# A linear-attention and soft-MoE kernel: the first key half in two 64-partition loads, the second as GpSimd's first load, phi on ScalarE's queue, and a last weight piece of three rows

## The chip, the core and the metric

One core of one Trainium2 chip. The core has TensorE (PE, matmuls), VectorE (DVE), ScalarE (ACT), GpSimd (POOL) and SyncE (SP, here only DMA issues), with 16 DMA engines shared by the queues of SP, ScalarE and GpSimd. The metric is device microseconds of one execution; times below are in microseconds unless they say otherwise.

## The reference

Two stages. The first is linear attention with a state per head (batch 4, 8 heads, 768 steps, head size 48); the second a soft mixture of experts over its output (3072 tokens of width 384, 8 experts of 4 slots, inner width 1024).

```python
for t in range(S):                       # r, k, v: [4, 8, 768, 48] fp32; w, u: [8, 48]
    cur = np.einsum('bhd,bhe->bhde', u[None] * kt, vt)
    y[:, :, t] = np.einsum('bhd,bhde->bhe', rt, state + cur)
    state = w[None, :, :, None] * state + np.einsum('bhd,bhe->bhde', kt, vt)
# x: y with heads joined, [3072, 384]
logits = x @ phi                         # [3072, 32]
d = softmax(logits, axis=0)              # over tokens
slot_input = d.T @ x                     # [32, 384]
slot_out[e] = relu(slot_input[e] @ w1[e]) @ w2[e]
out = softmax(logits, axis=1) @ slot_out # [3072, 384] fp32
```

## The kernel before

The sequence of 768 is cut into six chunks of 128 steps (`c` in names), and each chunk is worked with two pairs of batches (`bl`) and two halves of heads (`hf`). Every step is a named task of a class `Plan`: it has an engine, the tasks it depends on, and the buffers that it takes and frees. A long string `ORDER`, written out, says in which order the tasks are issued, in which buffer, and for tasks that may run on several engines on which (`/A` ScalarE, `/D` VectorE, `/P` GpSimd). Each engine runs its instructions in that order.

The names that matter here: `qk`, `qr`, `qv` copy a loaded key, r or v tensor into padded form (L222 is the copy on ScalarE, L224 that on VectorE); `tk`, `tr`, `tv` transpose it on TensorE (L376); `ek`, `er`, `ev` write it out of the accumulators with the decay tables (L386); `A`, `M` are the scores and their mask; `Y` the output of a chunk; `zt`, `ze` build the decay tables from `lnw`, the logarithm of w. After the last chunk, `h` and `ht` compute the experts' hidden layer, and `o00` to `o70` the second product, one expert after the other into one accumulator (L743).

Loads. All of r, k, v and the expert weights come through GpSimd's queue, which casts fp32 to bf16 on the way: `iL2` to `iL35` are halves (two batches) of a chunk's tensor, in the order k, r, v; then `iW0` to `iW7` the first weights and `iV0` to `iV7` the second. At most eight of these loads are outstanding: from `iL10` on each waits for the one eight before it. The second weights go into the buffers of r, k and v, once these have been copied. Only the first chunk's key (`iL0` and `iL1`) comes as fp32, by SP and ScalarE into `k0`, and the copies `qk00` and `qk01` cast it.

The last expert's second weight comes in two pieces: `Va7` with the first rows and `Vb7` with the last `YL` rows (of the eight that lie on each partition). `o70` uses the first piece; then `so1` copies the sum so far (on VectorE, L224). The first four output tiles (`p0` to `p3`, L788) start from `so1`, and have the last rows' share added by `pg0` to `pg3` (L795), which multiply the gathered hidden values `gG` (L756, evicted by `gE`) with `Vb7`'s rows directly. `o76` adds the same rows to the accumulator, and `so2` copies it for the tiles from the fifth on. Tiles are scaled and evicted (`oe`, L803 on ScalarE and L805 on VectorE) and stored by SP (`dm`, L811).

`WARM` puts filler matmuls (L826, results unused) behind named tasks; `fill` (L245) does so at the start.

Of the kernel before, what the change touches and what calls it, by code (L numbers as in the profile page):

```python
# [24 lines left out]
Y000:0,0 kn01:/D Y001:2 iL24 A011:0,0 iL25 s01:4,3,1 x000:/A M011 x001:/A tk20:0,0 iL26 ev10:/A X00:2,0 pr10:0/P
S111 A100:0,1 kn11:/A tk21:1 ek20 tr20:3,0 xT00:/A M100 bv10:5,2 qv2:0/A bv11:0,3 iL27 tr21:2 ek21 iL28 pr11:/D
bk20:1,1 iL29 vn10:/A er21 iL30 kn20:/A er20 s10:5,2,2 iL31 vn11:/A qk3:1/D tv20:1,0 iL32 S110 bk21:3,2 dv01:1 S200
D1:0,1 kn21:/A ev20:/D s11:4,5,3 S201 ds1:/A tv21:1 iL33 pr20:0/D Y011:3 iL34 ev21:/A Y010:0,1 S210 A101:0,0 iL35
pr21:/D l00:2 x010:/A bv20:4,0 iW0 M101 x011:/A D2:1,0 dv10:0 bv21:0,1 vn20:/A X01:3,1 lg00:/D ds2:/A A110:0,2 S211
vn21:/A qr3:0/D iW1 Y100:2,2 xT01:/A M110 iW2 Y101:4 x100:/A iW3 l01:1 s20:5,0,0 x101:/A lg01:/D iW4 mx0 X10:3,0  # L30
sb0:0/D S301 A111:0,1 ex0:0 iW5 S300 xT10:/A tk30:2,1 dv11:1 M111 c0:1 tk31:4 cT0:/A l10:0 ek31 qv3:1/A A200:0,0
iW6 Y111:5 ek30 iW7 Y110:3,3 M200 dv20:0 lg10:/A bk30:1,0 x111:/A s21:4,2,1 x110:/A kn30:/A tr30:0,1 dv21:1 S311
tr31:5 S310 X11:3,1 qk4:0/A A201:0,1 er30 tv30:1,1 M201 tv31:2 bk31:4,1 ev30:/A Y200:0,4 ev31:/D A210:0,2 xT11:/A
zu qr4:1/D Y201:1 x200:/D kn31:/A iV0 bv30:2,2 M210 bv31:3,3 x201:/A vn30:/A l11:0 X20:4,0 vn31:/D A211:0,0 xT20:/A
Y210:1,5 lg11:/D er31 tk40:2,0 M211 pr30:0/P x210:/A tk41:3 s30:0,4,2 qv4:0/A ek40 A300:0,1 Y211:5 ek41 iV1 l20:1
S401 bk40:2,2 x211:/A pr31:/P M300 tr40:3,0 lg20:/A kn40:/A X21:4,1 tr41:5 er40 xT21:/A A301:0,2 tv40:1,0 er41
qk5:1/A D3:2,1 M301 l21:3 iV2 bk41:4,0 tv41:5 pr40:0/P lg21:/A ds3:/A ev40:/D kn41:/A A310:0,0 s31:3,2,3 gm0
ev41:/A M310 gt0:1 dv30:0 qr5:0/A bv40:4,0 bv41:5,1 S410 mx2 iV3 vn40:/A mx1 Y301:3 S400 pr41:/P vn41:/A gr00
Y300:4,6 S411 A311:0,2 gd0 x300:/D x301:/A s40:0,1,0 M311 X30:5,0 dv31:1 tk50:2,1 xT30:/A D4:3,0 S500 A400:0,1 ek50
gb0:4 ds4:/A tk51:0 iV4 gx0 Y311:5 M400 sb1:1/P qv5:1/A gs0:/P Y310:3,7 l30:2 ek51 A401:0,2 dv40:0 tr50:4,1 x310:/A  # L40
x311:/D tr51:0 ex1:1 lg30:/D M401 X31:3,1 ge0 tv50:5,1 iV5 dp0:2 dv41:1 er50 ev50:/A er51 A410:0,0 xT31:/D
s41:4,5,1 pr50:0/P M410 c1:0 Y401:3 cT1:/A S511 A411:0,2 S501 tv51:0 iV6 M411 Y400:5,0 pr51:/P ev51:/A Y410:1,1
acc0 A500:0,1 S510 x401:/A Y411:2 x410:/A M500 x400:/A bv50:0,2 x411:/A D5:4,1 iVa7 X40:3,0 vn50:/D ds5:/A A501:0,0
sb2:0/D xT40:/A bv51:1,3 M501 dv50:0 l31:5 ex2:0 l40:2 vn51:/A X41:4,1 lg31:/D mx3 A510:0,2 lg40:/D sb3:1/D xT41:/A
c2:0 dv51:1 M510 Y500:3,2 cT2:/A Y501:5 ex3:1 l41:2 x500:/D A511:0,1 iVb7 x501:/A Y510:1,3 lg41:/A M511 X50:4,0
x510:/A c3:0 xT50:/A gm1 Y511:3 mx4 cT3:/A gt1:5 gl0:2 sb4:0/D x511:/D l50:1 ex4:0 gr10 X51:4,1 lg50:/A gr20 c4:0
gq1 gd1 xT51:/D cT4:/A gb1:3 gl1 F0 F1 gx1 gs1:/D gr21 ge1 gf1:/P l51:5 gq2 gg1 dp1:1 gd2 lg51:/D am1:/P mx5
sb5:1/D ex5:1 gb2:4 F2 F3 F4 acc1 gx2 gs2 gf2:/P ge2 gg2 am2:/D dp2:0 F5 F6 acc2 un1 un0 rv:3 h10:2 rw h11:5
hs10:/A h00:1 hs11:/D h01:4 hs00:/D ht1:0 hs01:/A c5:3 hT1:/D ht0:2 cT5:/A gG0:5 hT0:/D rs:1 gE0:/A gG1:4 rr o00:0
gE1:/A o10 o20 o30 o40 o50 F7 F8 F9 o60 F10 F11 F12 F13 F14 F15 o70 F16 F17 F18 so1 p0a:3 p0b:2 p1:5 pg0a pg0b pg1  # L50
oe0a oe0b o76 p2:1 oe1 dm00 pg2 so2:/A p3:4 dm01 pg3 oe2 p4:3 p5:2 oe3 p6:5 dm02 oe4 p7:0 p8:1 oe5 oe6 p9:4 dm03
p10:3 oe7 oe8 p11:2 dm04 p12:5 oe9 oe10 p13:0 dm06 p14:1 oe11 oe12 p15:4 p16:3 oe14 oe13 p17:5 dm10 p18:2 oe16 oe15
p19:1 p20:0 oe18 oe17 p21:3 dm14 p22:4 oe20 p23:2 oe21 oe22 oe23 oe19 dm20
"""


# [49 lines left out]
def kernel(  # L106
# [123 lines left out]
    def load_rkv(y):  # L230
        x, bb = divmod(y, 2)
        c, which = divmod(x, 3)
        src = (k, r, v)[which].rearrange("(bb bl) h (c p j) d -> c bb (bl h) p (j d)", bb=2, bl=2, p=RR, j=JJ)
        O(pool.dma_start(out=raw_t(x)[:, bb * JJ * D:(bb + 1) * JJ * D], in_=src[c, bb]))  # L234
# [16 lines left out]
    k_src = k.rearrange("(bb bl) h (c p j) d -> c bb (bl h) p (j d)", bb=2, bl=2, p=RR, j=JJ)
    O(act.dma_start(out=w_r[:, :, 0:D], in_=w[:, None, :].to_broadcast([H, 2, D])))
    for bb, q in ((0, sp), (1, act)):
        O(q.dma_start(out=k0[:, bb * JJ * D:(bb + 1) * JJ * D], in_=k_src[0, bb]))
    O(act.preload_act_table_set("natural_log_exp_and_others"))
# [8 lines left out]
    O(pool.affine_select(out=ident_f[:], in_=ident_f[:], compare_op=ALU.not_equal, fill=1.0, base=0,
                         pattern=[[-1, 128]], channel_multiplier=1))
    for t in rp_r:
        O(pool.memset(t[:, :, :, D:], 0.0))
# [592 lines left out]
```

## Time and profile before

| | |
|---|---|
| time, median of 3 runs | 117.49 (117.24 to 117.93) |
| the profiled execution | 117.38, span 115.6 from the first to the last instruction |
| TensorE busy | 98.7 (85%), granted clock 0.978 |
| VectorE busy | 89.8 (78%) |
| ScalarE busy | 76.7 (66%) |
| GpSimd busy | 66.4 (57%) |
| loaded by GpSimd's queue | 19.27 MB written |
| HBM | 39.38 MB read, 4.72 MB written |

A row of the timeline or of the groups gives start, duration, engine, source line, operation, what it writes and reads, and in brackets the idle time ahead of it with what ended it. A row of a table by stretches gives the stretch and its length, the busy time of PE, PEld (weight loads), DVE, ACT and POOL, each with its number of instructions, and then the granted clock, the mean busy share of the DMA engines and GB/s. A row of the DMA list gives the KB of one load and the median time from issue to landing.

### The profile page before, as it was taken

Reading aid. Unit: us, or ns where it says so; the run is one execution under the profiler, and the core shown is the slowest. Engines: PE = TensorE matmul, PEld = TensorE weight load, DVE = VectorE, ACT = ScalarE, POOL = GpSimd, SP = SyncE. Lnnn points to the kernel's source line nnn. Section 1 sums busy time; section 2 is a strip of 40 time slices with the busy share of each in tenths; the row PEclk is TensorE's granted clock in tenths of the full one; section 3 lists DMA queues with packets and bytes.
Section 4 is the critical chain, followed back from the end, with each engine's and each line's share of the span. In section 5 each row is a group of like instructions: output and inputs, shape, how many; then the busy total and the mean of one; then the engine's idle time right before and its main releaser. Section 6 shows DMA issues by size and latency. Waiting matters only on the chain.

```text
span 115.6 us, 3911 instructions
## 1 busy us (share of the span) xinstructions
PE 98.7 (85%) x1649; PEld 76.0 (66%) x1649; DVE 89.8 (78%) x178; ACT 76.7 (66%) x124; POOL 66.4 (57%) x85
## 2 busy tenths in 40 slices
...
DMA  2999999999999999999999999999999997059994
GB/s 36 268 197 206 207 205 210 205 206 208 208 210 201 229 219 208 218 219 212 210 220 215 210 220 210 214 219 212 215 223 208 217 209 149 17 208 404 408 438 174
DMA packets 9137, 25.08 MB, mean 217 GB/s; under 512 B 1184, under 2 KB 6176, under 8 KB 8992
## 3 DMA queue, kind: packets, MB, share of 16 engines
q0 software_dynamic: 7344, 19.27, 85.7%
...
q10 hardware_dynamic: 168, 0.40, 1.4%
...
HBM read 39.38 MB, written 4.72 MB: 381 GB/s over the span
## 4 chain that ended last, share of the span: by engine, by line
PE 48%; DMA 17%; DVE 11%; ACT 9%; POOL 5%; issue 3%; DVEq 0%; ACTq 0%; POOLq 0%
DMA w_all<-in_moe_w_dram 17%; PE pG L376 9%; PE pA L415 4%; PE pG L788 3%; ACT rp L222 3%; PE pG L397 3%; PE pA L826 3%; PE pG L743 3%; PE pG L633 2%; PE pG L716 2%; PE pG L516 2%; PE pG L551 2%; POOL w_all L237 2%; PE pG L490 2%; PE pG L496 2%
## 5 line engine op out<-in xcount | busy, mean ns | idle before, releaser
L421 DVE TENSOR_TENSOR AT<-pA,mask 128x1024 bf16<-128x1024 f32 x24 | 29.2, 1218 | 1.3 <-PE pA L415 1.1
L376 PE MATMUL pG<-ident,rp 128*128 128x128 bf16 x288 | 22.5, 235 | 2.6 <-DVE rp L224 2.4
L376 PEld LDWEIGHTS <-rp 128*128 128x128 bf16 x288 | 19.2, 106 | 3.8 <-issue 2.8
L428 POOL TENSOR_TENSOR pr<-kT,rT 128x1024 bf16<-128x1024 bf16 x8 | 17.0, 2130 | 5.1 <-DVE rT L386 4.6
L445 POOL TENSOR_TENSOR dv<-vn,ds 128x768 bf16<-128x768 bf16 x12 | 17.7, 1482 | 3.0 <-DVE sd L540 2.2
L222 ACT COPY rp<-raw 128x1536 bf16<-128x1536 bf16 x11 | 16.3, 1479 | 2.6 <-PE pG L376 2.3
L222 ACT COPY vT<-pG 128x1024 bf16<-128x1024 bf16 x8 | 8.0, 1015 | 5.2 <-PE pG L376 5.2
L474 DVE TENSOR_TENSOR S<-pG,W 128x384 bf16<-128x384 f32 x20 | 10.5, 548 | 0.5 <-PE pG L466 0.5
L803 ACT ACTIVATE w_all<-pG,rcs 128x384 f32<-128x384 f32 (+1 forms) x12 | 5.8, 587 | 6.1 <-PE pG L795 5.9
L415 PE MATMUL pA<-rT,kT 64*128 64x128 bf16 x192 | 9.5, 218 | 0.3 <-DVE AT L421 0.2
L386 DVE TENSOR_TENSOR kT<-pG,Tk 128x1024 bf16<-128x1024 bf16 x12 | 8.0, 684 | 1.7 <-PE pG L376 1.3
L222 ACT CAST x<-pG 128x384 bf16<-128x384 f32 x19 | 8.5, 487 | 0.8 <-PE pG L498 0.5
L222 ACT COPY xT<-pG 128x768 bf16<-128x768 bf16 x10 | 8.0, 804 | 1.3 <-PE pG L516 1.2
L496 PE MATMUL pG<-vn,AT 128*128 128x48 bf16 x192 | 8.7, 183 | 0.2 <-ACT kn L222 0.2
L222 ACT COPY vn<-pG 128x768 bf16<-128x768 bf16 x10 | 8.0, 815 | 0.9 <-PE pG L397 0.9
L805 DVE TENSOR_SCALAR w_all<-pG,rcs 128x384 f32<-128x384 f32 (+1 forms) x13 | 6.9, 596 | 1.6 <-PE pG L795 1.6
L234 POOL DMA_DIRECT2D raw<-in_v_dram x12 | 6.3, 537 | 3.1 <-DMA raw<-in_r_dram 3.0
L386 DVE TENSOR_TENSOR rT<-pG,Tr 128x1024 bf16<-128x1024 bf16 x12 | 7.9, 683 | 0.0
L498 PE MATMUL pG<-dv,ident 128*128 128x384 bf16 x24 | 7.7, 323 | 0.0
L222 ACT COPY kn<-pG 128x768 bf16<-128x768 bf16 x9 | 7.3, 812 | 0.5 <-PE pG L397 0.5
L415 PEld LDWEIGHTS <-kT 64*128 64x128 bf16 x192 | 5.7, 94 | 2.8 <-issue 1.1
L496 PEld LDWEIGHTS <-AT 128*128 128x128 bf16 x192 | 7.1, 96 | 0.4 <-issue 0.4
...
## 6 DMA issues: line engine op xcount, KB each, us to landing
...
raw<-in_r_dram POOLq DMA_DIRECT2D x12, 192.0 KB, 7.2
raw<-in_v_dram POOLq DMA_DIRECT2D x12, 192.0 KB, 6.8
raw<-in_k_dram POOLq DMA_DIRECT2D x10, 192.0 KB, 7.2
...
out_dram<-w_all SPq DMA_DIRECT2D x4, 192.0 KB, 2.0
```

The source lines that it names most:

```text
L222: O(act.copy(dst, src))
L234: O(pool.dma_start(out=raw_t(x)[:, bb * JJ * D:(bb + 1) * JJ * D], in_=src[c, bb]))
L376: O(pe.transpose(o[:, :, j, :], rp_r[W[rp]][:, jh * JH + j].rearrange("p b d -> p (b d)"), ident[:]))
L386: O(dve.tensor_mul(dst, src, (Tk, Tr)[which][:, None, jh].to_broadcast(BC)))
L415: O(pe.matmul(pA[:, bb, h4 * C:(h4 + 1) * C], kt[s, bl, h].rearrange("p a x -> p (a x)"), rt[s, bl, h].rearrange("p a x -> p (a x)"), star ...
L421: O(dve.tensor_mul(AT_r[W[f"AT{key}"]][:], pA[:].rearrange("p bb (h t) -> p bb h t", t=C), mask[:, None, None, :].to_broadcast([128, 2, H ...
L428: O(op(e).tensor_mul(pr_r[W[f"pr{c}"]][:, bl], kT_r[W[f"kT{c}"]][:, bl].rearrange("p h j x -> p h (j x)"), rT_r[W[f"rT{c}"]][:, bl].rearra ...
L445: O(op(e).tensor_mul(dv_r[W[f"dv{c}{bl}"]][:], vn_r[W[f"vn{c}{bl}"]][:], ds_r[W[f"ds{c}"]][:, bl, :, :, None].to_broadcast([128, H, 2, D])))
L474: O(dve.tensor_mul(S_r[W[new]][:, s], bank(kb[hf])[:, 0:HD].rearrange("p (h b d) -> p h b d", b=2, d=D), W128[:, s, :, None].to_broadcast( ...
L496: O(pe.matmul(o[:, z:z + D], AT_r[W[at]][:, bb, h4, :], vn[:, hf * H2 + h4, bb, :], start=(c == 0 and h4 == 0 and bb == 0), stop=False, sk ...
L498: O(pe.matmul(o[:, 0:HD], ident[:], dv_r[W[f"dv{c}{bl}"]][:, hf * H2:(hf + 1) * H2] .rearrange("p h b d -> p (h b d)"), start=False, stop= ...
L805: O(dve.tensor_scalar(out=dst, in0=src, scalar1=rcs[:, i:i + 1], scalar2=None, op0=ALU.mult))
```

## The change

The first key half comes in two loads of 64 partitions, one from SP and one from ScalarE, still as fp32. The second half becomes GpSimd's first load and is cast on the way, as the later ones. phi moves from SP's queue to ScalarE's, behind w. The padding memsets of `rp` move from GpSimd to VectorE. The last weight piece has three rows in place of two, so there are three gathered rows (`gG0` to `gG2`), and `o70` has five rows in place of six. The fillers behind `o50`, `o60` and `o70` go from 3, 6, 3 to 1, 5, 2. `ORDER` is a different one throughout, with copies, products and evictions divided differently between the engines. A dependency makes the second weight of the first expert wait for `qk01`, and another puts `o40` behind the gathers.

```diff
-WARM = [("gl1", 2), ("gb2", 3), ("dp2", 2), ("o50", 3), ("o60", 6), ("o70", 3)]
+WARM = [("gl1", 2), ("gb2", 3), ("dp2", 2), ("o50", 1), ("o60", 5), ("o70", 2)]
...
-zt3 zc iL6 zt1 ze3 iL7 zw:0 zt0 ze1 iL8 zb ze0 iL9 zt2 qk00:0/A za zd:/D ze2 qk01:/D iL10 tk00:0,0 tk01:1 qr0:1/A
+zt0 zc iL6 za ze0 iL7 zt1 iL8 qk00:0/D ze1 zt2 qk01:/A iL9 zt3 ze2 zw:0 tk00:0,0 iL10 zb ze3 tk01:1 qr0:1/D iL11
...
-    k0 = early[:, 2560:2560 + 2 * JJ * D]
+    k0 = early[:, 2560:2560 + JJ * D]
...
     k_src = k.rearrange("(bb bl) h (c p j) d -> c bb (bl h) p (j d)", bb=2, bl=2, p=RR, j=JJ)
+    for bl, q in ((0, sp), (1, act)):
+        O(q.dma_start(out=k0[64 * bl:64 * bl + 64], in_=k_src[0, 0, 8 * bl:8 * bl + 8]))
     O(act.dma_start(out=w_r[:, :, 0:D], in_=w[:, None, :].to_broadcast([H, 2, D])))
-    for bb, q in ((0, sp), (1, act)):
-        O(q.dma_start(out=k0[:, bb * JJ * D:(bb + 1) * JJ * D], in_=k_src[0, bb]))
+    O(act.dma_start(out=phi_f[:], in_=moe_phi.rearrange("(p mo) s -> p mo s", mo=nM)))
...
-    O(sp.dma_start(out=phi_f[:], in_=moe_phi.rearrange("(p mo) s -> p mo s", mo=nM)))
     O(sp.dma_start(out=u_r[:, :, 0:D], in_=u[:, None, :].to_broadcast([H, 2, D])))
...
+    for x in range(1, 6):
+        load_rkv(x)
+    fill(3)
     for t in rp_r:
-        O(pool.memset(t[:, :, :, D:], 0.0))
-    load_rkv(2)
-    load_rkv(3)
-    load_rkv(4)
-    load_rkv(5)
-    fill(3)
+        O(dve.memset(t[:, :, :, D:], 0.0))
...
-    YL = 2
+    YL = 3
...
-            P.add("i" + name, "POOL", lambda e, f=fns[kind], x=x: f(x), deps=[lands[n - 8]] if n >= 10 else [])
+            P.add("i" + name, "POOL", lambda e, f=fns[kind], x=x: f(x), deps=[lands[n - 8]] if n >= 9 else [])
...
-                    e, rp_r[W[rp]][:, :, bb, 0:D], k0[:, bb * JJ * D:(bb + 1) * JJ * D].rearrange("p (j d) -> p j d", j=JJ)),
+                    e, rp_r[W[rp]][:, :, bb, 0:D], (raw_t(0)[:, JJ * D:2 * JJ * D] if bb else k0).rearrange("p (j d) -> p j d", j=JJ)),
...
+    P.by["o40"]["deps"] += [f"gG{y}" for y in range(YL)]
...
-            P.by[f"i{kind}{e}"]["deps"] += [f"q{'krv'[x % 3]}{x // 3}" for x in (2 * e, 2 * e + 1) if x]
+            P.by[f"i{kind}{e}"]["deps"] += [f"q{'krv'[x % 3]}{x // 3}" for x in (2 * e, 2 * e + 1) if x] + ([] if e else ["qk01"])
```

GpSimd at the start of the program, before (`raw` is the buffer that the loads fill, `rp` the padded copies):

```order
L262 IOTA w_all 128x128
L264 AFFINE_SELECT ident_f<-ident_f 128x128
L267 MEMSET rp_77 128x32x16
L267 MEMSET rp_78 128x32x16
L234 DMA raw<-in_r_dram 128x1x768 x2
L234 DMA raw<-in_v_dram 128x1x768 x2
```

and now:

```order
L262 IOTA w_all 128x128
L264 AFFINE_SELECT ident_f<-ident_f 128x128
L234 DMA raw<-in_k_dram 128x1x768
L234 DMA raw<-in_r_dram 128x1x768 x2
L234 DMA raw<-in_v_dram 128x1x768 x2
```

A key load stands where the two memsets stood, and one load more is in the queue.

VectorE from the decay tables (L326, now L324) to the first products with them, before (`rp` from `w_all` is the fp32 key, `rp` from `raw` is r):

```order
L326 TENSOR_TENSOR w_all<-lnw,w_all 128x512 x3
L316 COPY wuT<-pA 128x16
L319 TENSOR_TENSOR ucol<-wuT 64x8 x2
L326 TENSOR_TENSOR w_all<-lnw,w_all 128x512
L312 COPY tokc<-pG_69 128x1
L313 TENSOR_SCALAR mask<-w_all,tokc 128x128
L224 CAST phi_s<-phi_f 128x96
L224 CAST rp_77<-w_all 128x16x48
L386 TENSOR_TENSOR kT_70<-pG_64,Tk 128x16x64
L386 TENSOR_TENSOR kT_70<-pG_65,Tk 128x16x64
```

and now:

```order
L324 TENSOR_TENSOR w_all<-lnw,w_all 128x512
L310 COPY tokc<-pG_69 128x1
L311 TENSOR_SCALAR mask<-w_all,tokc 128x128
L324 TENSOR_TENSOR w_all<-lnw,w_all 128x512
L224 CAST rp_77<-w_all 128x16x48
L324 TENSOR_TENSOR w_all<-lnw,w_all 128x512 x2
L314 COPY wuT<-pA 128x16
L317 TENSOR_TENSOR ucol<-wuT 64x8 x2
L224 COPY rp_78<-raw 128x2x16x48
L384 TENSOR_TENSOR kT_70<-pG_64,Tk 128x16x64
```

The copy of the key stands behind two tables in place of four and ahead of `wuT`, the copy of phi is gone from here (it is ScalarE's), and the copy of r stands ahead of the first product.

TensorE where the last weight piece is first used, before (from the last matmul on `so1`, which lies in a vT buffer, to the second tile half):

```order
L788 MATMUL pG_69<-vT_75,cT 128x384
L795 LDWEIGHTS vT_74
L795 MATMUL pG_67<-raw,vT_74 128x192
L795 LDWEIGHTS vT_74
L795 MATMUL pG_67<-raw,vT_74 128x192
L795 LDWEIGHTS vT_74
L795 MATMUL pG_66<-raw,vT_74 128x192
```

and now:

```order
L786 MATMUL pG_64<-vT_75,cT 128x384
L793 LDWEIGHTS vT_74
L793 MATMUL pG_67<-raw,vT_74 128x192
L793 LDWEIGHTS vT_74
L793 MATMUL pG_67<-raw,vT_74 128x192
L793 LDWEIGHTS vT_74
L793 MATMUL pG_67<-raw,vT_74 128x192
L793 LDWEIGHTS vT_74
L793 MATMUL pG_69<-raw,vT_74 128x192
```

Each part of a tile takes three matmuls on the last piece in place of two.

More of the change, by code (lines that the diff above doesn't have):

```diff
@@ L25 @@
[L25 to L53, printed above, removed]
+zt0 zc iL6 za ze0 iL7 zt1 iL8 qk00:0/D ze1 zt2 qk01:/A iL9 zt3 ze2 zw:0 tk00:0,0 iL10 zb ze3 tk01:1 qr0:1/D iL11
@@ new lines @@
+ek00 tr00:2,0 iL12 ek01 tr01:3 qv0:0/A iL13 er00 bk00:4,0 er01 iL14 bk01:5,1 pr00:0/D kn00:/A tv00:0,0 iL15
+A000:0,0 kn01:/D zd:/A pr01:/P qk1:1/A tv01:1 M000 ev01:/A tk10:2,1 qr1:0/D iL16 A001:0,1 tk11:3 ev00:/A ek10 iL17
+tr10:4,1 M001 iL18 qv1:1/A tr11:5 bv00:1,0 iL19 D0:2,0 er10 iL20 A010:0,2 vn00:/A bv01:0,1 er11 iL21 tv10:4,1
+ds0:/D vn01:/A ek11 dv00:0 tv11:1 s00:5,2,0 M010 ev10:/A s01:3,0,1 iL22 ev11:/A pr10:0/D Y000:4,0 iL23 S111
+A011:0,0 x000:/A bv10:1,2 iL24 pr11:/D Y001:0 iL25 M011 vn10:/A bv11:4,3 dv01:1 x001:/A D1:1,1 vn11:/A S100
@@ new lines @@
+A100:0,1 X00:0,0 S101 ds1:/A iL26 bk10:5,2 S110 xT00:/A Y010:4,1 iL27 M100 Y011:1 kn10:/A iL28 bk11:2,0 l00:3
+x011:/A qk2:0/D iL29 s10:0,5,2 qr2:1/A x010:/D dv10:0 A101:0,2 S200 tk20:1,0 M101 tk21:4 kn11:/A X01:0,1 iL30
+qv2:0/A Y100:2,2 iL31 S201 A110:0,0 ek20 iL32 Y101:5 M110 x100:/A iL33 tv20:1,0 xT01:/A dv11:1 tv21:2 x101:/A ek21
+A111:0,1 l01:0 ev21:/A X10:5,0 M111 iL34 xT10:/A s11:4,2,3 iL35 lg01:/D qk3:0/D lg00:/A iW0 Y111:0 ev20:/A mx0 S211
+tk30:5,1 iW1 sb0:0/D tk31:3 S210 ex0:0 bv20:2,0 iW2 ek30 qr3:0/A bv21:1,1 ek31 c0:4 tr20:5,0 iW3 cT0:/D tr21:3
@@ new lines @@
+vn31:/A tv40:2,0 ek40 tv41:0 ds3:/A ev40:/A X21:1,1 dv30:0 kn21:/D A301:0,0 ev41:/D tr40:3,0 xT21:/A M301 tr41:4
+dv31:1 qk5:1/A s21:5,2,1 er40 bv40:0,0 bv41:1,1 qr5:0/A er41 iV2 A310:0,1 S311 s30:3,4,2 pr40:0/P M310 vn41:/A
+Y300:2,6 vn40:/A S401 l21:1 A311:0,2 x300:/D lg21:/A bk31:4,1 ex1:1 pr41:/P S400 bk40:0,2 kn31:/A gm0 c1:1 bk41:2,0
+cT1:/A M311 tk50:3,1 kn41:/A gt0:4 tk51:1 iV3 kn40:/A gr00 D4:2,0 ek50 Y311:4 ds4:/A qv5:1/A S310 Y301:0 mx2
+A400:0,2 ek51 sb2:0/P Y310:2,7 dv40:0 M400 gd0 ex2:0 tv50:3,1 tv51:5 x311:/A x310:/A x301:/D gb0:1 A401:0,0 iV4
@@ new lines @@
+lg41:/A c3:1 X50:2,0 x510:/A cT3:/A gm1 Y511:4 xT50:/A mx4 gt1:5 sb4:0/P x511:/D gl0:3 ex4:0 gr10 l50:0 gq1 X51:1,1
+gr20 gd1 lg50:/A c4:2 gb1:4 xT51:/D cT4:/A gx1 gl1 gs1:/D l51:5 F0 ge1 gr21 gf1:/P F1 lg51:/A gq2 gg1 dp1:0 mx5 gd2
+am1:/P sb5:1/P gb2:1 F2 acc1 ex5:1 F3 gx2 gs2 F4 gf2:/P ge2 c5:4 gg2 dp2:2 am2:/D cT5:/A F5 F6 acc2 un1 rv:3 un0
+rs:5 rw h01:0 rr h00:1 hs01:/D h10:4 hs00:/A h11:2 hs10:/A ht0:3 hs11:/A hT0:/D ht1:5 gG1:0 hT1:/D o00:1 o10 gE1:/D
+o20 o30 gG0:4 gG2:2 o40 gE0:/A gE2:/D o50 F7 o60 F8 F9 F10 F11 F12 o70 F13 so1 F14 p0a:3 p0b:5 p1:0 pg0a pg0b pg1
```

17 lines of the change are left out of this document (13 added, 4 removed).

## The prediction

> **What bounds the kernel now.** The page comes first: the DMA row of its forty slices, and the queues.
>
> ```profile
> span 115.6 us, 3911 instructions
> DMA  2999999999999999999999999999999997059994
> q0 software_dynamic: 7344, 19.27, 85.7%
> q10 hardware_dynamic: 168, 0.40, 1.4%
> ```
>
> The DMA engines are full from the second slice to slice 33 (about 3 to 95 us), nearly all of it in the queue that GpSimd feeds. The profiled execution took 117.38 us for a span of 115.6, so 1.78 us lie around the span; it is 0.11 under the median of 117.49. TensorE is also busy nearly all of that time, so the second question is which of the two ends last. The timeline of GpSimd says when the two pieces of the last expert's second weight were issued, the DMA list how long each took to land, and the table by stretches how the engines ran dry.
>
> ```profile
> 73.67 0.59 POOL L240 DMA_DIRECT2D raw<-in_moe_w_dram  x1
> 79.34 0.59 POOL L240 DMA_DIRECT2D raw<-in_moe_w_dram  x1
> ...
> raw<-in_moe_w_dram POOLq DMA_DIRECT2D x1, 576.0 KB, 25.0
> raw<-in_moe_w_dram POOLq DMA_DIRECT2D x1, 192.0 KB, 20.3
> ...
> 97.00:98.00 1.00, 1.00 (x12) 0.40 (x5) 0.00 (x0) 0.00 (x0) 0.00 (x0) 1.00 0.61 112
> 98.00:99.00 1.00, 0.97 (x10) 0.31 (x8) 0.00 (x0) 0.00 (x0) 0.00 (x0) 1.00 0.24 43
> 99.00:100.00 1.00, 1.00 (x11) 0.41 (x6) 0.56 (x1) 0.00 (x0) 0.00 (x0) 1.00 0.04 6
> ```
>
> The six-row piece (Va7) lands at 73.67 + 25.0 = 98.67, the two-row piece (Vb7) at 79.34 + 20.3 = 99.64. Both had been in the queue for over 20 us, so their landing is set by what lies ahead of them in the DMA engines, not by their issue. The share falls over more than two microseconds (0.61, 0.24, 0.04): a few engines finish last, and they decide. Now TensorE at the same place, from the timeline and, for the last four rows, the chain of waits.
>
> ```profile
> 97.25 1.47 PE L826 MATMUL pA<-ones 128*128 128x512 bf16 x6
> 98.75 0.50 PE L743 MATMUL pG<-raw,rT 128*32 128x384 bf16 x6
> 99.28 0.56 DVE L224 CAST vT<-pG 128x384 bf16<-128x384 f32 x1 [5.19 <-PE pG L743]
> 100.22 0.82 PE L795 MATMUL pG<-raw,vT 128*128 128x192 bf16 x6
> 102.50 5.87 DVE L805 TENSOR_SCALAR w_all<-pG,rcs 128x384 f32<-128x384 f32 x11 [0.73 <-PE pG L795]
> ...
> 100.38 0.66 PE pG L795 x6
> 101.04 0.27 PE pG L743 x2
> 101.58 0.33 PE pG L795 x2
> 102.06 0.33 PE pG L795 x2
> ```
>
> The six matmuls that need Va7 (o70) start at 98.75, 0.08 after it landed. The chain names the filler matmuls of L826 before them, but those only pass the time. From there the path is o70, the copy so1 (L224), three short matmuls, and at 100.22 the first matmul on Vb7, 1.55 after Va7's landing and 0.58 after Vb7's. Behind it the first four output tiles come as TensorE finishes them (VectorE waited 0.73 for the fourth), and then the stores run:
>
> ```profile
> 102.00:103.00 1.00, 1.00 (x8) 0.59 (x6) 0.50 (x1) 0.93 (x2) 0.00 (x0) 1.00 0.82 297
> 104.00:106.00 2.00, 1.92 (x10) 0.77 (x8) 2.00 (x5) 2.00 (x6) 0.00 (x0) 1.00 1.00 382
> ```
>
> Before 104 the DMA engines have room (0.82), after it none (1.00). So a delay up to the fourth tile moves the end, and later tiles wait for stores. The end is set by the landing of the last weight and by TensorE's work from there to the fourth tile.
>
> **The change part by part. The start.** These rows of the DMA list, the timeline and the stretches show what moves.
>
> ```profile
> w_all<-in_k_dram SPq DMA_DIRECT2D x1, 384.0 KB, 4.5
> w_all<-in_k_dram ACTq DMA_DIRECT2D x1, 384.0 KB, 5.4
> w_r<-in_w_dram ACTq DMA_DIRECT2D x1, 3.0 KB
> u_r<-in_u_dram SPq DMA_DIRECT2D x1, 3.0 KB
> ...
> 1.33 0.98 POOL L267 MEMSET rp<- 128x512 bf16 x2
> 1.38 0.62 ACTq L254 DMA_DIRECT2D w_all<-in_k_dram  x1
> 2.03 1.28 ACT L255 ACT_TABLE_LOAD   x1 [2.03 <-issue]
> 3.37 0.18 ACT L288 ACTIVATE lnw<-pA 128x8 f32<-128x8 f32 x1
> 9.78 4.53 PE L376 MATMUL pG<-ident,rp 128*128 128x128 bf16 x41 [2.43 <-DVE rp L224]
> ...
> 8.70 0.52 POOL L234 DMA_DIRECT2D raw<-in_v_dram  x1 [2.08 <-DMA raw<-in_r_dram]
> 13.50 0.51 POOL L234 DMA_DIRECT2D raw<-in_r_dram  x1 [0.48 <-DMA raw<-in_k_dram]
> ...
> 2.00:2.25 0.25, 0.25 (x2) 0.15 (x1) 0.14 (x3) 0.22 (x1) 0.25 (x1) 1.00 0.52 74
> 2.50:2.75 0.25, 0.25 (x2) 0.00 (x0) 0.25 (x5) 0.25 (x1) 0.25 (x1) 1.00 0.55 123
> 2.75:3.00 0.25, 0.25 (x1) 0.00 (x0) 0.24 (x2) 0.25 (x1) 0.25 (x2) 1.00 0.57 160
> 3.00:3.50 0.50, 0.50 (x4) 0.44 (x3) 0.23 (x1) 0.44 (x2) 0.50 (x2) 1.00 0.92 369
> ```
>
> *Price of a cast half.* GpSimd's later loads each wait for an earlier one to land, first at 8.70 and, five landings on, at 13.50: (13.50 - 8.70) / 5 = 0.96 us for each half of 192 KB once the engines are full. Queue q0 gives nearly the same: 85.7% of 115.6 for 19.27 MB is 1.01 for a half of 0.197 MB.
>
> *Price of an fp32 half.* It reads the same bytes as a cast half, so 0.96 at least; q10, which is one such half and w_r, took 1.4% of 115.6 = 1.62 at most.
>
> *How many engines.* In before each key half has a source whose outer dimension is 16. The two new loads have one of 8 heads. The DMA list gives a landing time for every load except w_r and u_r, and those two are the only ones with an outer dimension of 8. I read this as loads that don't complete on all sixteen engines, and take it that the new key loads run on eight, the same eight for both. Those eight then carry the fp32 packets that they carried before (two halves over sixteen are as many for each as one half over eight), and GpSimd's extra half on top: +0.96. The other eight get rid of what these keep. The rule for this is in the Trainium skill, "DMA: Bandwidth & Descriptors", section "Rules for kernel authors": a DMA uses no more engines than the slowest dimension of its access pattern allows, so an outer dimension of 8 holds it to eight; by that the sum below stands, and the missing landings agree with it.
>
> *Idle time at the start.* Shares of 0.52, 0.55, 0.57 and 0.92 in the stretches above leave 0.12 + 0.11 + 0.11 + 0.04 = 0.38 us idle. With both key loads issued first and GpSimd's first load 0.98 earlier (no memsets ahead), the loaded engines fill it: -0.38, at worst 0. The last weight then lands 0.96 - 0.38 = 0.58 later, if one of the loaded eight is last.
>
> *ScalarE.* It issues a third DMA ahead of the table load, some 0.56 to 0.62 as its neighbours, so the table load ends near 3.9 and lnw (3.37) slips by half a microsecond. The memsets on VectorE lie under that. In return the key's second copy no longer stands behind the u table, and the first transposes (9.78) can start two microseconds earlier. But the new order puts the copy of r ahead of the first multiply on VectorE, so most of this is lost again to r's landing. What remains is TensorE's lead, which ends where it waits for Va7. I cost it at nothing; without that cover, a later loop costs its lateness one for one.
>
> **The tail.** Three rows instead of two in the last piece: it costs the queue 0.48 more after Va7 (half of the spacing 99.64 - 98.67 = 0.97), so Va7 lands 0.48 earlier for it: 98.67 + 0.58 - 0.48 = 98.77. From there to the first matmul on Vb7 1.55, less one matmul of o70 (0.50 / 6 = 0.08): 100.24. Vb7 lands at 99.64 + 0.58 = 100.22, and with the same 0.06 to 0.08 behind it the matmul starts at 100.28. That is +0.06 against 100.22.
>
> Behind it each of the four tiles has a third matmul: 0.66 / 2 = 0.33 for the first two, 0.27 / 2 = 0.13 for o75, 0.165 each for the third and fourth: +0.79 up to the fourth tile. Since the stores have room until then, I take it whole. If only the first store counted it would be 0.17.
>
> The fillers: nine before o70 become six, 1.47 / 6 = 0.25 each, so TensorE could be there 0.75 sooner, less the third gate matmul (its row stands with the last rival). Va7 lands later than that, so this gives nothing.
>
> Sum: +0.06 + 0.79 = +0.85, that is 118.23 against the profiled 117.38, and 118.3 beside the median. Bounds of this case: 0.06 + 0.17 = +0.23 and 0.06 + 0.38 + 0.79 = +1.23, so 117.7 to 118.7.
>
> **The rivals.** *Sixteen engines, equal prices.* If both loads spread over all engines, an fp32 half goes and a cast half comes at the same 0.96, and only the idle 0.38 is gained. Vb7 lands at 99.26, the first matmul on it starts at 99.32, 0.90 sooner, and less 0.79 that is -0.11: 117.4. For it: the bytes read are the same. Against it: the missing landings. The same holds, roughly, if the engine that ends last is one of the unloaded eight. The Trainium skill has a sentence for this too, in the same page and section: two transfers to disjoint partition halves aren't worth it, since both spray over all sixteen engines; no run here shows such a pair, and by that rule the time would be this one.
>
> *Sixteen engines, a dear fp32 half (faster).* If the fp32 half costs what q10 shows, 1.62, its removal is worth 0.66 more at the start: -0.77, 116.7. It decides for faster once an fp32 half costs over 1.44. Against it: q10's time contains waiting for packets of the other queues.
>
> *TensorE late.* Every row of the order is new, and TensorE is busy through it:
>
> ```profile
> 92.69 0.37 PE pG L756
> ...
> sum 68.00, PE 66.06 PEld 55.65 DVE 64.57 ACT 55.47 POOL 52.08; mean PE 4.72 PEld 3.97 DVE 4.61 ACT 3.96 POOL 3.72
> ```
>
> Of the 68 us from 20 to 88, 66.06 are TensorE's, so extra waits in the loop show one for one once the lead at Va7 is used up. That lead is small: 0.75 less the third gate matmul (0.37, the chain's row of L756) is 0.38, and of the two microseconds at the start r's landing leaves perhaps 0 to 0.6 (an estimate), so 0.4 to 1.0 in all. A loop 1.5 longer would put 0.5 to 1.1 on top of the forecast: 119.2.
>
> **How the numbers follow.** Eight engines: 0.50. Sixteen with equal prices, or the last engine an unloaded one: 0.20. Sixteen with a dear fp32 half: 0.18. TensorE late: 0.12. I count 0.5% (0.59 us) as the least that a measurement tells from no change. Faster is the dear half, 0.18. Within 0.5% (116.90 to 118.08) is the case of equal prices and the lower part of the first, 0.20 + 0.12 = 0.32. Slower is the rest, 0.38 + 0.12 = 0.50. The range runs from 116.7 to 118.9: it leaves out most of the last case and the lower edge of the dear half. The likeliest case alone has 117.7 to 118.7.
>
> **What would show it.** In the profile after: Vb7's landing (issue and time to landing) near 100.2, Va7's near 98.8, o70 right behind Va7 with a wait before it; no landing time for the two 64-partition loads; four tiles 0.79 longer. A landing of Vb7 at 99.3 or before makes the eight engines wrong. A first output store that begins sooner than now although Vb7 lands later makes the tail wrong. o70 well behind Va7's landing means that TensorE is late.

## The result, and the profile after

| | before | after |
|---|---|---|
| time, median | 117.51 | 120.84 (4 runs, 119.82 to 121.01) |
| ratio to before | | 1.0265, 95% interval 1.0232 to 1.0299 |
| the profiled execution | 117.38, span 115.6 | 120.78, span 119.0 |
| granted clock of TensorE | 0.978 | 0.979 |
| last weight piece lands | 99.64 | 102.43 |

The kernel is 3.3 us slower by the medians, 3.1 by the ratio, far outside the range forecast (116.7 to 118.9). Here and below a time is the median of all executions of a kernel, and its ratio leaves out the ones that lie over 1.5% above its fastest (one each in e3_issue_early, e4_two_rows, e6_w_first_sixteen and the kernel before). The pages show where to look: the forty slices of the GB/s that the DMA engines moved, in the kernel before, and the same with the engines' share in the kernel after.

```profile
GB/s 36 268 197 206 207 205 210 205 206 208 208 210 201 229 219 208 218 219 212 210 220 215 210 220 210 214 219 212 215 223 208 217 209 149 17 208 404 408 438 174
```

```profile
DMA  1899998999999999999999999999999997069992
GB/s 22 180 209 207 207 207 137 177 163 201 207 207 207 218 222 207 225 207 222 207 224 207 224 207 222 209 219 212 215 216 213 216 207 139 11 228 400 410 444 107
```

The digits of the share hide it (they stop at 9). The GB/s show it: slices 7 to 9, about 18 to 27 us, carry 137, 177 and 163 in place of 205 to 210. The table by stretches gives the same place; its first row is of the kernel before, where the share of full DMA engines is 1.16 and not 1, the others are of the kernel after:

```profile
20.00:25.00 5.00, 4.46 (x83) 3.67 (x83) 5.00 (x8) 4.74 (x7) 4.60 (x7) 1.00 1.16 206
...
17.00:20.00 3.00, 2.34 (x42) 1.96 (x40) 3.00 (x4) 3.00 (x4) 3.00 (x4) 1.00 0.96 170
20.00:23.00 3.00, 3.00 (x68) 2.88 (x66) 3.00 (x6) 2.71 (x4) 2.54 (x5) 1.00 1.05 160
23.00:26.00 3.00, 2.71 (x57) 2.18 (x55) 3.00 (x5) 2.67 (x4) 3.00 (x6) 1.00 1.06 145
```

Why the engines have too little to move there is told by GpSimd's rows of the timeline, first of the kernel before, then of the kernel after:

```profile
13.50 0.51 POOL L234 DMA_DIRECT2D raw<-in_r_dram  x1 [0.48 <-DMA raw<-in_k_dram]
14.41 0.51 POOL L234 DMA_DIRECT2D raw<-in_v_dram  x1 [0.40 <-DMA raw<-in_r_dram]
15.23 2.12 POOL L428 TENSOR_TENSOR pr<-kT,rT 128x1024 bf16<-128x1024 bf16 x1 [0.30 <-DVE pr L428]
17.30 0.56 POOL L234 DMA_DIRECT2D raw<-in_v_dram  x1
```

```profile
13.50 0.51 POOL L234 DMA_DIRECT2D raw<-in_r_dram  x1 [0.46 <-DMA raw<-in_k_dram]
16.61 2.13 POOL L426 TENSOR_TENSOR pr<-kT,rT 128x1024 bf16<-128x1024 bf16 x1 [2.60 <-DVE pr L426]
18.68 1.11 POOL L234 DMA_DIRECT2D raw<-in_v_dram  x2
```

Up to 13.50 the loads are issued as before. Then the next load (iL16) stands behind the product pr01, GpSimd waits 2.60 for VectorE's part of the same product, and no load is issued from 14.0 to 18.7. VectorE is late because the decay tables are, and they are late because w is. In the timeline at the start:

```profile
0.74 1.37 ACTq L253 DMA_DIRECT2D w_all<-in_k_dram  x1
2.15 0.34 ACTq L254 DMA_DIRECT2D w_r<-in_w_dram  x1
7.70 0.24 PE L284 MATMUL pA<-ident_f,w_r 8*128 8x8 f32 x1 [4.57 <-DMA w_r<-in_w_dram]
7.98 0.18 ACT L286 ACTIVATE lnw<-pA 128x8 f32<-128x8 f32 x1 [3.79 <-PE pA L284]
```

w, 3 KB, was the first load on ScalarE's queue and now stands behind a part of the first key half. TensorE waits 4.57 for it, and lnw comes at 7.98 in place of 3.37.

At the other end, the last pieces' issues and times to landing, then the rows of TensorE and VectorE that answer to those of before:

```profile
77.44 0.59 POOL L240 DMA_DIRECT2D raw<-in_moe_w_dram  x1
79.83 0.60 POOL L240 DMA_DIRECT2D raw<-in_moe_w_dram  x1
...
raw<-in_moe_w_dram POOLq DMA_DIRECT2D x1, 480.0 KB, 23.6
raw<-in_moe_w_dram POOLq DMA_DIRECT2D x1, 288.0 KB, 22.6
```

```profile
101.03 0.48 PE L741 MATMUL pG<-raw,rT 128*32 128x384 bf16 x5 [0.57 <-DMA raw<-in_moe_w_dram]
...
102.49 1.15 PE L793 MATMUL pG<-raw,vT 128*128 128x192 bf16 x9
...
105.36 5.87 DVE L803 TENSOR_SCALAR w_all<-pG,rcs 128x384 f32<-128x384 f32 x11 [1.06 <-PE pG L793]
```

Va7 lands at 77.44 + 23.6 = 101.04 and o70 starts there, after a wait of 0.57 on the DMA. Vb7 lands at 79.83 + 22.6 = 102.43 and the first matmul on it starts 0.06 later. So the landing of the last weight still sets the end. The fourth tile is 105.36 - 102.50 = 2.86 later than before, the span 3.4. The 0.54 between lies behind the start of the fourth tile, where the stores run. From there to the end the profiled runs took 13.1 in the kernel before, e5_before_w_late and f3_before_three_rows, 13.6 to 13.7 in the kernel after and most of its variants, 14.0 in f1_first_sixteen_two_rows and 14.2 in f2_old_order_new_load. These are single executions. The new order with the loads of before (e8_old_loads, 13.7) and the new loads with the order of before (f2_old_order_new_load) both have the longer time, and no run isolates the cause.

### The profile page after: what moved, and what is told of

It reads as the page before. It is cut to its first block, busy times and chain, and to the rows that moved or that the text cites. A ratio compares the mean times of both kernels' runs of the same rounds, so it can differ in the third digit from the quotient of the medians.

```text
span 119.0 us, 3897 instructions
## 1 busy us (share of the span) xinstructions
PE 98.1 (82%) x1648; PEld 75.6 (64%) x1651; DVE 90.7 (76%) x176; ACT 79.6 (67%) x129; POOL 61.3 (52%) x84
## 4 chain that ended last, share of the span: by engine, by line
PE 44%; DMA 24%; ACT 10%; DVE 8%; issue 3%; ACTq 1%; POOL 1%; DVEq 0%; POOLq 0%
DMA raw<-in_moe_w_dram 20%; PE pG L374 12%; PE pG L395 6%; DMA w_r<-in_w_dram 5%; PE pA L413 4%; PE pG L786 3%; ACT rp L222 3%; PE pG L488 3%; PE pG L494 3%; PE pG L496 2%; ACT vT L222 2%; ACT vn L222 2%; DVE w_all L803 2%; PE pG L793 2%; PE pG L460 1%
## 5 line engine op out<-in xcount | busy, mean ns | idle before, releaser
L374 PE MATMUL pG<-ident,rp 128*128 128x128 bf16 x288 | 21.2, 230 | 1.9 <-ACT rp L222 1.7
L374 PEld LDWEIGHTS <-rp 128*128 128x128 bf16 x288 | 18.5, 103 | 3.2 <-ACT rp L222 1.9
L222 ACT COPY rp<-raw 128x1536 bf16<-128x1536 bf16 (+1 forms) x13 | 18.4, 1440 | 0.8 <-ACT Tr L328 0.8
L222 ACT COPY vn<-pG 128x768 bf16<-128x768 bf16 x12 | 9.6, 820 | 4.0 <-PE pG L395 4.0
L426 POOL TENSOR_TENSOR pr<-kT,rT 128x1024 bf16<-128x1024 bf16 x5 | 10.6, 2126 | 2.9 <-DVE pr L426 2.6
L222 ACT COPY vT<-pG 128x1024 bf16<-128x1024 bf16 x11 | 11.1, 1032 | 0.8 <-PE pG L374 0.8
L234 POOL DMA_DIRECT2D raw<-in_r_dram x12 | 6.5, 557 | 2.7 <-DMA raw<-in_k_dram 2.7
L234 POOL DMA_DIRECT2D raw<-in_v_dram x12 | 7.1, 609 | 1.0 <-DMA raw<-in_r_dram 1.0
L395 PE MATMUL pG<-ident,vT 128*128 128x128 bf16 x96 | 7.0, 219 | 0.1
```

The source lines that it names most:

```text
L222: O(act.copy(dst, src))
L374: O(pe.transpose(o[:, :, j, :], rp_r[W[rp]][:, jh * JH + j].rearrange("p b d -> p (b d)"), ident[:]))
L395: O(pe.transpose(bank_b(kb)[:, h * C:(h + 1) * C], src[:, bl, h].rearrange("p a x -> p (a x)"), ident[:]))
L426: O(op(e).tensor_mul(pr_r[W[f"pr{c}"]][:, bl], kT_r[W[f"kT{c}"]][:, bl].rearrange("p h j x -> p h (j x)"), rT_r[W[f"rT{c}"]][:, bl].rearra ...
```

## The experiments

Ratios are to the kernel before on the same chip, with 95% intervals. A landing comes from the one profiled run of a kernel; such runs lie up to 0.6 from their median in most of these kernels (1.2 in e3_issue_early, 1.4 in e4_two_rows), so sizes are taken from the ratios and the landings say where.

**w ahead of the key load.** The kernel after, with one line moved:

```diff
+    O(act.dma_start(out=w_r[:, :, 0:D], in_=w[:, None, :].to_broadcast([H, 2, D])))
     for bl, q in ((0, sp), (1, act)):
         O(q.dma_start(out=k0[64 * bl:64 * bl + 64], in_=k_src[0, 0, 8 * bl:8 * bl + 8]))
-    O(act.dma_start(out=w_r[:, :, 0:D], in_=w[:, None, :].to_broadcast([H, 2, D])))
```

> The changed kernel with one edit: on ScalarE's queue w is issued ahead of its key load, as in before. Theory Q (queue: w lands late behind the key load, all of the start is late, GpSimd's product stands late in front of the next loads, the DMA engines run dry around 18 to 28 us): w lands near 2.3, lnw near 4 in place of 7.98, GpSimd's second pr near 15 in place of 16.61, no slice with less than 195 GB/s between 18 and 30, the last piece lands near 99.6 to 100.2 in place of 102.4; 117.7 to 118.5 us. Theory E (eight engines: the two key loads crowd half of the engines and so delay all): the loads still run on eight engines, so the last piece lands at 101.5 or later and the time stays over 120. Theory O (the new order is slower by itself): no weight is waited for at the end and the time stays over 119.5.

118.69, just above the range expected, ratio 1.0099 (1.0072 to 1.0126): 2.0 us of the 3.1 come back. In its rows lnw is at 3.90, GpSimd's product at 14.37 with a short wait, and slices 7 to 9 carry 192, 200 and 204 GB/s:

```profile
3.90 0.18 ACT L286 ACTIVATE lnw<-pA 128x8 f32<-128x8 f32 x1
14.37 2.12 POOL L426 TENSOR_TENSOR pr<-kT,rT 128x1024 bf16<-128x1024 bf16 x1 [0.61 <-DVE pr L426]
78.00 0.60 POOL L240 DMA_DIRECT2D raw<-in_moe_w_dram  x1
...
raw<-in_moe_w_dram POOLq DMA_DIRECT2D x1, 288.0 KB, 22.2
```

Vb7 lands at 100.20, which is close to the 100.22 that the prediction had for it.

**w behind the key load, in the kernel before.** The opposite edit, alone, in the old kernel with its full 128-partition loads:

```diff
-    O(act.dma_start(out=w_r[:, :, 0:D], in_=w[:, None, :].to_broadcast([H, 2, D])))
     for bb, q in ((0, sp), (1, act)):
         O(q.dma_start(out=k0[:, bb * JJ * D:(bb + 1) * JJ * D], in_=k_src[0, bb]))
+    O(act.dma_start(out=w_r[:, :, 0:D], in_=w[:, None, :].to_broadcast([H, 2, D])))
```

> The kernel before with one edit: ScalarE issues w behind its key half (a load of 128 partitions on all engines), everything else as before. Theory Q (a small load behind a key load on the same queue lands with or after it, and the decay tables wait for it): w lands at 4.5 to 6.8 in place of 2.24, lnw at 5 to 7 in place of 3.37, the products start 1.5 to 3 us later, GpSimd's loads from about the fourteenth on are issued late, 118.5 to 120.5 us. Rival (the late w matters only with the changed order, or the key load on eight engines is needed for it): 117.3 to 117.9.

120.41, ratio 1.0284 (1.0224 to 1.0345): the place of one 3 KB load costs the old kernel as much as the whole change does. The timeline and the stretches show the same chain, stronger:

```profile
7.41 0.24 PE L286 MATMUL pA<-ident_f,w_r 8*128 8x8 f32 x1 [4.28 <-DMA w_r<-in_w_dram]
17.97 2.12 POOL L428 TENSOR_TENSOR pr<-kT,rT 128x1024 bf16<-128x1024 bf16 x1 [3.65 <-DVE pr L428]
...
GB/s 32 270 203 207 206 207 161 123 190 197 206 204 195 196 218 206 226 206 222 210 218 215 212 222 210 219 206 228 201 231 204 220 210 183 14 182 388 413 417 199
```

**The key half by columns.** Two loads of all 128 partitions, half a row each, so that the outer dimension is 16; w stays behind.

```diff
-    for bl, q in ((0, sp), (1, act)):
-        O(q.dma_start(out=k0[64 * bl:64 * bl + 64], in_=k_src[0, 0, 8 * bl:8 * bl + 8]))
+    for jh, q in ((0, sp), (1, act)):
+        z = slice(jh * JH * D, (jh + 1) * JH * D)
+        O(q.dma_start(out=k0[:, z], in_=k_src[0, 0, :, :, z]))
```

> The changed kernel with the first key half cut along the free dimension (columns, two loads of 128 partitions) and not into two times 64 partitions: each load has an outer dimension of 16, w still behind the key load on ScalarE's queue. Theory E: all sixteen engines share the loads, a landing time appears in the list, the early difference goes, 117.5 to 118.5 us. Theory Q: w still stands behind a key load, now with half the bytes per engine, and lands at about 4.5 to 6 in place of 7.6; lnw gains 1.5 to 3 us, the dry stretch gets shorter but need not go; 118.5 to 120. Theory O: no change, 120.5 to 121.

118.71, ratio 1.0092 (1.0065 to 1.0118). The two key loads now have landing times in the DMA list, and w comes almost 3 us sooner though it stands at the same place in the queue:

```profile
w_all<-in_k_dram SPq DMA_DIRECT2D x1, 192.0 KB, 3.1
w_all<-in_k_dram ACTq DMA_DIRECT2D x1, 192.0 KB, 3.7
...
4.91 0.24 PE L285 MATMUL pA<-ident_f,w_r 8*128 8x8 f32 x1 [1.78 <-DMA w_r<-in_w_dram]
```

No slice from 18 to 27 us falls below 206 GB/s in it. So this edit and w first overlap: each alone takes back some 2 us, since loads on eight engines also double what lies ahead of w on each of these engines. What the eight engines cost by themselves needs w first.

**Both: w first and columns.** The two edits above together.

> The changed kernel with w issued first on ScalarE's queue and the first key half cut by columns, so that both key loads have an outer dimension of 16: against the run with w first alone (118.69) it tells what the eight engines cost. Theory E small: the last piece lands 0.3 to 0.6 sooner than there (100.20), 118.1 to 118.4 us. If the eight engines cost nothing, 118.6 to 118.8.

117.72, ratio 1.0021 (0.9985 to 1.0056), that is 0.78% (give or take 0.45) or 0.92 us under e1_w_first, more than the 0.3 to 0.6 expected. The last piece, from its issue and its time to landing:

```profile
76.47 0.60 POOL L240 DMA_DIRECT2D raw<-in_moe_w_dram  x1
...
raw<-in_moe_w_dram POOLq DMA_DIRECT2D x1, 288.0 KB, 22.8
```

It lands at 99.27, 0.93 before that of e1_w_first. This is the price of the eight engines: the prediction had 0.96. That there are eight can be read in the traces, which keep the times of the semaphore updates by which a load reports its landing. SP's key load has sixteen of them here, from 3.24 to 3.74. The 64-partition one of the kernel after has nine, one at 1.97 and eight from 3.95 to 5.08, and so the list can give it no landing:

```profile
w_all<-in_k_dram SPq DMA_DIRECT2D x1, 192.0 KB
w_all<-in_k_dram ACTq DMA_DIRECT2D x1, 192.0 KB
```

**How a late w reaches the end.** If it does so through GpSimd's load standing behind a product, issuing the load first should undo it. In the order of the kernel after, w late:

```diff
-... zd:/A pr01:/P qk1:1/A ... qr1:0/D iL16 A001:0,1 ... ek10 iL17
-tr10:4,1 M001 iL18 ...
+... zd:/A iL16 iL17 iL18 pr01:/P qk1:1/A ... qr1:0/D A001:0,1 ... ek10
+tr10:4,1 M001 ...
```

> The changed kernel with three of GpSimd's loads (iL16 to iL18) moved ahead of its second product pr, which waits for VectorE; the start as changed, w late. Theory Q, second half (the loss comes from the DMA engines running dry, not from the late computing): the dry stretch at 18 to 21 goes, the last piece lands 1.5 to 2.7 sooner (99.7 to 100.9), and the time falls to 118.5 to 119.5, where TensorE, late by the start, takes over as the bound. If instead the late computing alone makes the end, the time stays at 120.5 to 121 although the DMA engines stay full.

121.38, ratio 1.0295 (1.0234 to 1.0357): a miss, nothing came back. The stretches show that the empty time has only moved on, and GpSimd's row says to where: the next product, dv00, waits 2.02 for VectorE, with the loads behind it.

```profile
17.00:20.00 3.00, 2.32 (x39) 1.77 (x37) 3.00 (x4) 3.00 (x4) 3.00 (x3) 1.00 1.15 205
20.00:23.00 3.00, 3.00 (x67) 2.88 (x64) 3.00 (x7) 2.54 (x3) 0.98 (x3) 1.00 1.15 207
23.00:26.00 3.00, 2.70 (x58) 2.18 (x55) 3.00 (x6) 2.67 (x5) 3.00 (x5) 1.00 1.07 168
26.00:29.00 3.00, 2.92 (x66) 2.55 (x64) 3.00 (x5) 2.69 (x6) 3.00 (x5) 1.00 1.07 180
...
22.62 1.47 POOL L443 TENSOR_TENSOR dv<-vn,ds 128x768 bf16<-128x768 bf16 x1 [2.02 <-DVE ds L224]
```

So every load was then put ahead: from pr01 on, each of GpSimd's load tokens up to iL35 takes the place of the one three before it, w still late.

```diff
-... pr01:/P ... iL16 ... iL17 ... iL18 ... iL32 ... iL33 ... iL34 ... iL35
+... iL16 iL17 iL18 pr01:/P ... iL19 ... iL20 ... iL21 ... iL35
```

> The kernel after, with w still behind the key load, but every one of GpSimd's loads from the 17th stands three loads earlier among its products, so that none of the first products stands ahead of a load that could be issued. If the empty DMA queue is how the late w reaches the end: lowest slice of the DMA engines above 185 GB/s, Vb7 lands within 0.4 of the 100.2 that w first gave, time 118.4 to 119.2. If the late w reaches the end through the engines' own work (products late, TensorE behind), the landing comes back and the time does not: 120 to 121, o70 with a wait on an engine or TensorE busy up to it.

119.89, ratio 1.0183 (1.0137 to 1.0230), 0.82% (give or take 0.57) under the kernel after, but 0.84% (give or take 0.54), 1.0 us, over w first: between the two theories. The landing did come back, to within 0.5 of w first; from 18 to 27 us the page's GB/s stay at 202 to 207, and the last pieces land at 78.38 + 20.9 = 99.28 and 80.78 + 19.9 = 100.68:

```profile
GB/s 22 168 207 206 205 207 207 202 207 210 202 209 203 221 212 216 218 216 215 214 216 209 220 211 220 213 216 217 214 219 212 211 200 58 6 235 404 411 438 108
78.38 0.59 POOL L240 DMA_DIRECT2D raw<-in_moe_w_dram  x1
80.78 0.60 POOL L240 DMA_DIRECT2D raw<-in_moe_w_dram  x1
...
raw<-in_moe_w_dram POOLq DMA_DIRECT2D x1, 480.0 KB, 20.9
raw<-in_moe_w_dram POOLq DMA_DIRECT2D x1, 288.0 KB, 19.9
```

But TensorE is no longer waiting for them. The timeline of TensorE has no DMA wait there, and o70 (the five matmuls of L741) starts 1.24 behind its piece:

```profile
98.90 0.51 PE L741 MATMUL pG<-raw,rT 128*32 128x384 bf16 x8
99.34 1.25 PE L825 MATMUL pA<-ones 128*128 128x512 bf16 x5
100.52 0.50 PE L741 MATMUL pG<-raw,rT 128*32 128x384 bf16 x5
```

A late w thus has two ways to the end. The longer is the empty DMA queue; when it is closed, the engines' own lateness shows next, at o70, where five fillers that used to pass idle time (1.25) now lie on the path. This edit itself also delays GpSimd's second dv product (27.53 against 25.82 in the kernel after), and in its profiled run w could be used only at 8.30, 0.60 later than in that of the kernel after, so how much of that lateness belongs to w alone is not settled.

**The third row.** Two rows again, in the kernel after (the token `o75` becomes `o76`, `gG2` and `gE2` go):

```diff
-    YL = 3
+    YL = 2
```

> The changed kernel with a last piece of two rows (YL = 2, without the third gather and its eviction), all else as changed. By the terms of the prediction the longer piece gives 0.5 between the landing and the first matmul on it and costs 0.6 to 0.8 up to the fourth tile: 120.5 to 120.8, at most 0.3 faster. If the three-row tail is what the kernel lost by, 118 to 119.

120.01, ratio 1.0197 (1.0162 to 1.0232): 0.68%, give or take 0.48, faster than the kernel after, where at most 0.3 us had been expected. Then the same with w first:

> The changed kernel with w first and a last piece of two rows: against the run with w first alone (118.69) it tells what the three-row piece costs or gives. By the prediction's terms the first matmul on the piece comes 0.48 later and the fourth tile 0.6 to 0.8 sooner behind it: 118.4 to 118.6 us. If the longer piece pays, 118.8 to 119.2.

118.29, ratio 1.0072 (1.0049 to 1.0094), 0.27% (give or take 0.35) under e1_w_first, which can't be told from nothing. And three rows alone in the kernel before:

```diff
-    YL = 2
+    YL = 3
-... gE0:/A gG1:4 rr o00:0 gE1:/A o10 ... oe0b o76
+... gE0:/A gG1:4 rr gG2:5 o00:0 gE1:/A gE2:/D o10 ... oe0b o75
```

> The kernel before with a last piece of three rows (a third gather, o75), nothing else. By the prediction's own steps for the tail, without the eight engines: the first matmul on the piece moves from 100.22 to 99.64 + 0.07 = 99.71, 0.51 sooner, and four tiles cost 0.79 more, +0.28: 117.8, ratio 1.0024. By what two rows were worth with w first (0.40): 117.9, ratio 1.0034. Rival (only the first store counts): 0.51 - 0.17, that is 117.15, ratio 0.997.

118.06, ratio 1.0044 (1.0012 to 1.0077): +0.52 us, with 0.28 forecast by the prediction's steps. Its timeline at the first use of the piece:

```profile
78.94 0.59 POOL L240 DMA_DIRECT2D raw<-in_moe_w_dram  x1
98.46 0.50 PE L743 MATMUL pG<-raw,rT 128*32 128x384 bf16 x5
99.94 1.15 PE L795 MATMUL pG<-raw,vT 128*128 128x192 bf16 x9
...
raw<-in_moe_w_dram POOLq DMA_DIRECT2D x1, 288.0 KB, 20.7
```

Vb7 lands at 99.64, as before, but the matmul comes 0.30 behind it and not 0.07: without the eight engines' delay, o70 and so1 set the start. The gain of the earlier start is 0.28 then, not 0.51. From there the fourth tile takes 2.93 (it starts at 102.87) in place of 2.28, so 0.65 more, not 0.79: by these rows +0.37, which the measured 0.52, give or take 0.38, doesn't contradict.

**The order and the loads, apart.** The kernel after with the whole start of before (both key halves fp32 in 128 partitions, w first, phi on SP, memsets on GpSimd), so that the new order, three rows and the fillers are left:

```diff
-    k0 = early[:, 2560:2560 + JJ * D]
+    k0 = early[:, 2560:2560 + 2 * JJ * D]
-    for bl, q in ((0, sp), (1, act)):
-        O(q.dma_start(out=k0[64 * bl:64 * bl + 64], in_=k_src[0, 0, 8 * bl:8 * bl + 8]))
+    for bb, q in ((0, sp), (1, act)):
+        O(q.dma_start(out=k0[:, bb * JJ * D:(bb + 1) * JJ * D], in_=k_src[0, bb]))
...
```

> The changed kernel with the whole start as in before (both key halves fp32 on all engines from SP and ScalarE, w first, phi on SP, the rp memsets on GpSimd), so only the order, the three-row piece and the fillers are new. Theory Q with the tail's price: the loss by w's place is gone and the tail's 0.1 to 0.4 stays, 117.6 to 118.1 us. Theory O (the new order is slower by itself): 118.4 to 119.2, with the last piece landing well before it is used, or with loads issued late.

117.97, ratio 1.0062 (1.0039 to 1.0085). f3_before_three_rows has the same rows in the old order and 1.0044, so the new order with its fillers costs 0.18%, give or take 0.40: nothing that can be told. The reverse, the new loads in their good form (w first, columns) with the old order, the old fillers and two rows:

> The order, the fillers and the two-row piece of the kernel before, with the second key half as GpSimd's first load, the first half by columns from SP and ScalarE, w first, phi on ScalarE's queue, memsets on VectorE. Theory (a cast half and an fp32 half cost the DMA engines the same, and only the idle time at the start is gained): Vb7 lands 0.2 to 0.4 sooner than 99.64, time 117.1 to 117.3, ratio 0.997. Rival 1 (the fp32 half was dear): 116.7 or less. Rival 2 (the copy of the second half now waits for a GpSimd load that lands with the first ones, and the first products come late): 117.6 or more, the first transposes later than 9.78.

117.76, ratio 1.0017 (0.9988 to 1.0046). Vb7 lands at 78.59 + 20.9 = 99.49:

```profile
78.59 0.59 POOL L240 DMA_DIRECT2D raw<-in_moe_w_dram  x1
...
raw<-in_moe_w_dram POOLq DMA_DIRECT2D x1, 192.0 KB, 20.9
```

That is 0.15 sooner than before, within the scatter, and the time has no gain from it, where 117.1 to 117.3 had been expected. A late second half isn't the reason: the first transposes start at 8.35, before at 9.78. Last, all repairs in the new order: w first, columns, two rows.

> The kernel after with w ahead of the key load, the key half cut by columns into two 128-partition loads, and two rows in the last piece; the new order and the cast second half are all that is left of the change in the loads. Theory (the three costs add): 117.72 of the kernel with the first two undone, less the 0.40 that the third row cost with w first: 117.3, ratio 0.998. Rival (with the landing early, TensorE's lead in the new order is used up, so the third row no longer costs): 117.7, o70 with a wait on an engine ahead of it and not on a DMA.

117.66, ratio 1.0005 (0.9981 to 1.0030). The 117.3 by which the three costs would add up was missed; the time is that of the rival, but not for its reason, since o70 still waits 1.06 for the DMA. Nothing that was tried beats the kernel before; the change with its three costs taken out equals it.

## Why the prediction was wrong

The sign was right, the size was not, and the failing step is the paragraph *ScalarE*. It priced ScalarE's queue by the time to issue its three DMAs ("lnw (3.37) slips by half a microsecond") and "I cost it at nothing". It never asked when w lands once it stands behind a key half on the same queue. lnw slipped by 4.6 us, not 0.5. Taken back (e1_w_first) this step is worth 1.66% of the time before (give or take 0.43), 2.0 us; put into the old kernel alone (e5_before_w_late) it costs 2.84%.

The second half of that paragraph failed with it: "What remains is TensorE's lead, which ends where it waits for Va7". Late work was to be hidden by TensorE's lead, and TensorE's lead did hold in the kernel after: o70 waited for the DMA. But late work has a way to the end around that lead. What the prediction left out is that GpSimd's products stand in one line with GpSimd's loads. A late product holds up the issue of loads, and so moves the landing itself; the DMA engines that were taken as always full ran at 145 to 170 GB/s for nine microseconds. That this is not the only way is shown by f4_loads_ahead: with the landing back at 100.68, 1.0 us over w first stayed.

Point by point, the other steps:

- *The landing sets the end.* Right in the kernel after (0.57 of waiting at o70, 0.06 from Vb7's landing to its first matmul, where 0.06 to 0.08 was forecast).
- *Eight engines, +0.96.* Right: 0.92 us, give or take 0.53, between e1_w_first and e6_w_first_sixteen, and 0.93 in the landing. Of the two rules of the Trainium skill, "DMA: Bandwidth & Descriptors", section "Rules for kernel authors", the one on the slowest dimension, by which these loads keep to eight engines, agrees with that. The other, that two transfers to disjoint partition halves spray over all sixteen, does not: the same bytes cut by columns were 0.92 us better.
- *Idle time filled, -0.38.* Open. e6_w_first_sixteen lies 0.41% (give or take 0.42), 0.5 us, under e8_old_loads, which has the same order and rows and the loads of before, and its last piece lands at 99.27 and not at 77.42 + 22.4 = 99.82; that fits. In the old order with two rows f2_old_order_new_load is 0.17% (-0.12 to 0.46) over before, and its last piece lands 0.15 sooner; that doesn't. Its stores took longer, as said above, which could hide such a gain. The sum itself was loose: it took 1 for the share of full engines, and from 20 to 88 us that share is 1.03 to 1.16.
- *The dear fp32 half* (116.7, a chance of 0.18) is out: e6_w_first_sixteen, f1_first_sixteen_two_rows and f2_old_order_new_load remove one fp32 half, none is faster than before, and their last pieces land 0.15 to 0.37 sooner, not the 0.66 + 0.38 = 1.04 of that case. The case of equal prices on sixteen engines (117.4) is nearest to what they show, at 117.66 to 117.76.
- *The tail.* Behind Vb7 the fourth tile came at 105.36 - 102.49 = 2.87, before at 102.50 - 100.22 = 2.28: +0.59, with 0.79 forecast. Its net price without eight engines was 0.52, give or take 0.38, where 0.28 was forecast; the earlier start gave less than forecast, since o70 and so1, not Vb7, then set it.
- *TensorE late* (119.2, a chance of 0.12). Not in the kernel after, where the landing was later still; in f4_loads_ahead, once the landing had come back, it was what ended last.

With w first, the forecast for the rest would have been 118.3, and the kernel so built measured 118.69, inside the range. That it is so near is luck in part, as the -0.38 in it stays open.
